# A three-stage Trainium2 kernel: eleven weight-half subtractions of the second group moved from GpSimd to VectorE, and to a later place

## The chip, the cores and the metric

The kernel runs on one core of a Trainium2 chip. The metric is the device time of one execution in microseconds (us). The engines are named as the profile names them: PE is TensorE (matmuls), PEld its weight load, DVE is VectorE, ACT is ScalarE, POOL is GpSimd, SP is the engine whose queue issues most DMAs. A "q" behind a name (SPq) is that engine's queue.

## What is computed

Three layers follow each other. The first is a linear attention with a decaying state over 2 batch rows, 8 heads, 768 steps and head size 48; the second and third are feed-forward layers of width 384 and 1024. In the excerpt the first two functions matter, since the change lies where they overlap.

```python
def _attn_ref(r, k, v, w, u):
    state = np.zeros((B, H, D, D))
    for t in range(S):
        cur = np.einsum('bhd,bhe->bhde', u[None] * kt, vt)
        y[:, :, t] = np.einsum('bhd,bhde->bhe', rt, state + cur)
        state = wt[:, :, :, None] * state + np.einsum('bhd,bhe->bhde', kt, vt)

def _moe_ref(x, mu_k, mu_r, w_k, w_v, w_r):
    xk = mu_k * x + (1.0 - mu_k) * x_prev
    xr = mu_r * x + (1.0 - mu_r) * x_prev
    k = np.maximum(xk @ w_k, 0.0)
    v = k * k @ w_v
    r = 1.0 / (1.0 + np.exp(-(xr @ w_r)))
    return r * v

def _moe2_ref(x, w_in, g_ln, w_sg, b_sg, w_out):
    h = gelu(x @ w_in); u, v = halves(h)
    v_s = w_sg @ normalised(v) + b_sg
    return x + (u * v_s) @ w_out
```

## The kernel before

The 1536 tokens are cut into four groups of 384 (half a batch row each). The attention of a group is done in four units, each a pair of heads over three chunks of 128 steps: units 0 to 3 are group 0, units 4 to 7 group 1, units 8 to 11 group 2. This text calls the ninth unit unit 8, as the code counts.

A unit has four stages on TensorE. S (`attn_sc`) transposes the scaled keys into `kt_ps`, from unit 8 on also sums the u-weighted products over a head into `ab`, and makes the scores `sc`. K (`attn_kv`) multiplies values with the keys' copy `kt` into `kv`. Y (`attn_y`) applies the masked scores `am`, and Z (`attn_z`) adds the carried state. Between them VectorE multiplies the masks in (`am<-sc`, two instructions, one for each head), forms `ru<-ab,uvt`, and steps the state (`zt`, `zcar`); ScalarE copies the keys out of PSUM (`kt<-kt_ps`, called the key eviction here) and scales the state into `sblk` and `scar`. `ab` and `kv` use the same PSUM buffer, so a unit's `kv` matmuls start only when `ru<-ab` has read it.

The second layer's products of a group stand between the stages of the next group's units: eight products k (`moe1_k`, here k0 to k7), three r, then three v in four parts each. In group 0 the weights are used whole. From group 1 on each weight and each input is a high half and a low half, and a product is three passes (high·high, low·high and high·low). For that the weights are split once, in `split1` and `split_to`: ScalarE copies the high half (`wh`, line 314) and another engine subtracts it from the full weight (`wkl`, `wrl`, `wvl`, line 315). The eight k weights are split on VectorE, the three r and eight v weights on GpSimd, all called from `moe1_v` when the last product of group 0 is written down. The k halves are needed by k0 of group 1, the r halves at its first r, the v halves at its first v.

Each k product is evicted by ScalarE with three instructions, `kr<-mm` (line 673), `kh<-kr` (686) and the square `kr<-kr` (687), and VectorE subtracts `kl<-kr,kh` (688). The inputs of the products are made in `moe1_prep` by `dx` on ScalarE (640) and VectorE (642), high halves `xkh` and `xrh` on ScalarE (645) and low halves `xkl` and `xrl` on VectorE (646).

The order on TensorE is written out by hand: a `plan` lists every stage and product, and `TS` gives the time that the plan expects for each. VectorE, ScalarE and the DMA queues are ordered by a scheduler from the priorities that `with at(time)` sets and from what is ready; `tc.issue_after(ins)` puts what a block issues on the engine of `ins` behind it in that engine's order, without a wait. Each engine runs its instructions in order. The low halves share a ring of buffers (tag `wl`) with the full weights, so a low half reuses the buffer of a weight split two places before it, and the third layer's weights (`stg<-w_in` loaded by SP, `top` on ScalarE, `wf` on VectorE) follow in the same ring. Three staging buffers hold these loads.

Of the kernel before, what the change touches and what calls it, by code (L numbers as in the profile page):

```python
# [13 lines left out]
AF = mybir.ActivationFunctionType  # L14
# [10 lines left out]
NP = H // 2  # L25
PW = 2 * D
HP = 64
PR = HP + D
WL = CG * (CH + 1) + 1
KM = DM // 128  # L30
# [30 lines left out]
NVN = 8  # L61
# [9 lines left out]
def emit(tc, tin, nin, vt, consts, ucp, pars, b_sg, w_k, w_v, w_r, w_in, w_sgT, w_out, outT):  # L71
    nc = tc.nc
    V, A, PL, PE, SP = nc.vector, nc.scalar, nc.gpsimd, nc.tensor, nc.sync
# [94 lines left out]
    TS, TE = {}, {}  # L168
# [53 lines left out]
    def wide(i):  # L222
        return i >= NP * N_DIAG
# [4 lines left out]
    def load_uvt(i):  # L228
        src = tin[subs[i // NP][0] * NP + i % NP]
        for q in rows(i == NP * N_DIAG):  # L230
            with at(TS["Y", i] - 9):
                SP.dma_start(uvts[q], src[q, WL + 2 * G:WL + 3 * G])
# [44 lines left out]
    def pair():  # L277
        return pl["w"].tile([128, 2 * WT + 2], U32 if early["n"] < N_EARLY else F32R, name="wh", tag="wh", bufs=NW1 // 2 + 1)
# [33 lines left out]
    def split_to(hi, lo, full, dl, e):  # L312
        with at(dl):
            i = A.activation(hi, full, AF.Copy).ins  # L314
            e.tensor_tensor(lo, full, hi.bitcast(F32), ALU.subtract)  # L315
        return i

    def full1(nm, i, shape):
        wt[nm, i] = (pl["w"].tile(shape, F32, name="w" + nm, tag="wl", bufs=NW1 + SPARE),)

    def split1(nm, i, dl, e=PL):
        if not split_ops[0]:
            return
        full = wt[nm, i][0]
        shape = list(full.shape)
        lo = pl["w"].tile(shape, F32R, name="w" + nm + "l", tag="wl", bufs=NW1 + SPARE)
        if early["hi"] % 2 == 0:
            early["t"] = pair()
        o = early["hi"] % 2 * WT
        early["hi"] += 1  # L330
        hi = early["t"][:, o:o + WT].rearrange("p (c f) -> p c f", c=shape[1])
        ins = split_to(hi, lo, full, dl, e)
        wt[nm, i] = (hi, lo)
        return ins
# [62 lines left out]
    st = {}  # L397
# [36 lines left out]
    def attn_sc(i):  # L434
        tS, tK, tY = TS["S", i], TS["K", i], TS["Y", i]
        s = st[i]
        nc_ = subs[i // NP][2]
        kt_ps = pq.tile([128, 512], F32, name="kt_ps", tag="kt", bufs=1)
        for c in range(nc_):
            PE.transpose(kt_ps[:, c * PR:(c + 1) * PR], s["kp"][:, c], ident[0:PR, 0:PR])  # L440

        def sums(bs):
            s["bs"] = bs
            for c in range(nc_):
                PE.matmul(bs[:, 2 * c:2 * c + 2], s["ruk"][:, c * CH:(c + 1) * CH], hm, start=True, stop=True)  # L445

        if i >= NP and not wide(i):
            sums(kt_ps[:, nc_ * PR:nc_ * PR + 2 * nc_])
        kt = pa.tile([128, nc_, PR], F32, name="kt", tag="ktsb")
        with at(tS + 0.5):  # L450
            A.activation(kt, kt_ps[:, 0:nc_ * PR].rearrange("p (c d) -> p c d", d=PR), AF.Copy)
        s["kt"] = kt
        am = pa.tile([128, 2, nc_, CH], F32, name="am", tag="am", bufs=B_AM)
        sc = [pq.tile([128, 512], F32, name="sc", tag="sc", bufs=2)[:, 0:nc_ * CH].rearrange("p (c t) -> p c t", t=CH)
              for _ in range(2)]
        if wide(i):
            ab = pq.tile([128, 512], F32, name="ab", tag="kv", bufs=1)[0:PR, 0:nc_ * CH]
            PE.matmul(ab, hblk, s["ruk"], start=True, stop=True)  # L458
        for c in range(nc_):
            for h in range(2):  # L460
                hs = slice(h * HP, h * HP + D)
                PE.matmul(sc[h][:, c], s["kp"][hs, c], s["rp"][hs, c], start=True, stop=True)  # L462
        if wide(i):
            with at(tK - 1.6):
                V.tensor_tensor(s["ruk"], ab, uvts, ALU.mult)
            if i + 1 < NU:
                load_uvt(i + 1)
            self_am(i, am, sc, tY)
            return
        if i < NP:  # L470
            sums(head["bs"][0][:, 0:2 * nc_])
        self_am(i, am, sc, tY)
        vb = pa.tile([128, nc_, 2, D], F32, name="vb", tag="vb", bufs=2)
        with at(tK - 1.6 if i >= NP else tY - 1.4):
            bh = s["bs"].rearrange("p (c h) -> p c h", h=2)[:, :, :, None].to_broadcast([128, nc_, 2, D])
            V.tensor_tensor(vb, uv[i].rearrange("p c (h d) -> p c h d", h=2), bh, ALU.mult)
        s["vb"] = vb

    def self_am(i, am, sc, tY):
        s = st[i]  # L480
        nc_ = subs[i // NP][2]
        for h in range(2):
            with at((TS["K", i] - 1.4 if i >= NP else tY - 1.2) + 0.4 * h):
                mask = cmask[:, None, :].to_broadcast([128, nc_, CH])
                s["am"] = V.tensor_tensor(am[:, h], sc[h], mask, ALU.mult).ins  # L485
        s["at"] = am
# [173 lines left out]
    def mm_tile():  # L660
        mmp["n"] += 1
        if mmp["q"] is not None and mmp["n"] % 8 >= 3:
            return mmp["q"].tile([128, 512], F32, name="mn", tag="mn", bufs=5)
        return pm.tile([128, 512], F32, name="mm", tag="mm", bufs=3)
# [35 lines left out]
    def moe1_v(s, j, q):  # L700
        g, c0, n = subs[s]
        js = slice(j * 128, (j + 1) * 128)
        if q == 0:
            m1[s, "ps"] = mm_tile()[:, 0:n * CH]
        ps = m1[s, "ps"]
        fs = range(q * KF // VQ, (q + 1) * KF // VQ)
        mm(ps, [(part(wt["v", f], slice(None), 0, js), m1[s, "k", f]) for f in fs], q == 0, q == VQ - 1)
        if q < VQ - 1:
            return
        with at(TE["v", s, j] - 0.5):  # L710
            V.tensor_tensor(x2[g][:, j, c0 * CH:(c0 + n) * CH], ps, m1[s, "r", j], ALU.mult)
        if s == NAT["r"] - 1 and j == KM - 1 and split_ops[0]:
            with tc.issue_after(st[2 * NP - 1]["ev"]):
                for f in range(KF):
                    hi = split1("k", f, TS["k", s + 1, f], V)
            with tc.issue_after(hi):
                for f in range(KM):
                    split1("r", f, TS["r", s + 1, f])
                for f in range(NVN):
                    split1("v", f, TS["v", s + 1, 0] + f * 0.49)  # L720

    m2 = {}

# [229 lines left out]
    def products(i):  # L953
        for _ in head["prep", i]:
            pass
# [14 lines left out]
    for n, key in enumerate(keys[:n_in]):  # L970
        kd, g = key[0], key[1]
# [40 lines left out]
        if kd == "S" and g >= UPIN - 1 and g + 1 < NU:  # L1012
            with tc.issue_after(st[g]["am"]):
                products(g + 1)
        if kd == "Z" and g >= NP and g + 2 < UPIN:
            prep(g + 2)
        elif kd == "Z" and g >= NP and g + 2 < NU:
            with tc.issue_after(st[g]["zt"]):
                scans(g + 2)
# [98 lines left out]
```

## Time and profile before

| what | us |
|---|---|
| median of 3 runs | 346.44 |
| lowest and highest of the 3 | 345.92, 348.27 |
| the profiled execution's own time | 346.58 |
| its span in the profile | 344.8 |

The span runs from the first to the last instruction that the profiler saw. The granted clock of TensorE was 0.998 of full speed over the span. A row of the timeline gives start, duration, engine, line, operation, output and inputs, count, and in brackets the engine's idle time before it with the work that the profile says ended it. That last name is an inference: where the named work had long been done, it was another.

### The profile page before, as it was taken

The page shows a single profiled execution, that of the slowest core. Times are in us where ns is not written, and L with a number is a line of the kernel's source. Part 1 is how long each engine was busy: PE and PEld are TensorE (multiplying, and loading weights), DVE is VectorE, ACT ScalarE, POOL GpSimd, SP SyncE. Part 2 cuts the span into 40 slices and gives each one's busy share as a digit, 9 for nine tenths or more (in the row PEclk, how much of TensorE's full clock was granted, in tenths as well). Part 3 has the DMA queues.
Part 4 walks back from the last instruction along what each step waited for, and adds up shares of the span by engine and source line. Part 5 has one row for each costly group of instructions (what it writes and reads, how often), then busy time and mean ns, then how long its engine had stood idle before and what let it go on. Part 6 is the DMA issues. An engine that isn't in the chain of part 4 may idle for free.

```text
span 344.8 us, 5996 instructions
## 1 busy us (share of the span) xinstructions
PE 332.2 (96%) x2179; PEld 289.9 (84%) x2179; DVE 243.7 (71%) x531; ACT 182.6 (53%) x430; POOL 32.9 (10%) x56
## 2 busy tenths in 40 slices
PE   7999999999978999999999999999999999999993
PEld 3776577676767889888899999989999999999992
DVE  5997899789968883699439652498989732645531
ACT  3474986537789751777438892868353206211100
POOL 3000000001750000000004053000000000000000
PEclk9999999999999999999999999999999999999999
DMA  8788963754224430011013423613330010100012
GB/s 223 191 286 252 310 181 110 202 134 129 96 61 135 117 108 19 18 27 44 19 63 94 136 86 107 216 25 80 78 82 20 1 70 0 46 25 0 2 73 75
DMA packets 23750, 33.97 MB, mean 99 GB/s; under 512 B 3504, under 2 KB 18032, under 8 KB 23712
## 3 DMA queue, kind: packets, MB, share of 16 engines
q1 hardware_dynamic: 21568, 31.09, 31.3%
q10 hardware_dynamic: 2144, 2.41, 2.4%
q8 instruction: 19, 0.31, 0.4%
q14 instruction: 19, 0.16, 0.2%
HBM read 28.77 MB, written 2.36 MB: 90 GB/s over the span
## 4 chain that ended last, share of the span: by engine, by line
PE 85%; DVE 5%; ACT 4%; DMA 3%; issue 1%; POOL 0%; SPq 0%; DVEq 0%; ACTq 0%; POOLq 0%
PE mm L606 41%; PE mn L606 27%; PE sc L462 4%; PE y L545 3%; PE y L559 3%; ACT wh L314 2%; DMA wh<-w_r 2%; PE kv L501 2%; PE y L548 1%; PE kt_ps L440 1%; PE ab L458 1%; DMA uw<-tin 1%; PE mm L937 1%; PE kt_ps L445 1%; DVE dx L642 1%
## 5 line engine op out<-in xcount | busy, mean ns | idle before, releaser
L594 ACT ACTIVATE gah<-gt 128x384 fp32r<-128x384 f32 x16 | 8.4, 526 | 44.4 <-DVE gt L787 44.4
L640 ACT ACTIVATE dx<-xx,par 128x384 f32<-128x384 f32 x22 | 13.3, 611 | 22.0 <-DMA xx<-yo 19.9
L527 ACT ACTIVATE sblk<-zt,pf 48x48 f32<-48x48 f32 x60 | 19.8, 331 | 9.4 <-DVE zt L511 6.6
L606 PE MATMUL mm<-kh,wh 128*128 128x384 f32 x64 | 22.1, 346 | 0.0
L606 PE MATMUL mm<-kh,wvl 128*128 128x384 f32 x64 | 21.6, 337 | 0.0
L606 PE MATMUL mm<-kl,wh 128*128 128x384 f32 x64 | 21.5, 336 | 0.0
L606 PE MATMUL mm<-xkh,wh 128*128 128x384 f32 x57 | 20.3, 357 | 0.0
L606 PE MATMUL mn<-wsh,vl 128*128 128x384 f32 x60 | 20.0, 334 | 0.0
L606 PE MATMUL mn<-wsh,vh 128*128 128x384 f32 x60 | 20.0, 334 | 0.0
L606 PE MATMUL mn<-wsl,vh 128*128 128x384 f32 x60 | 20.0, 334 | 0.0
L688 DVE TENSOR_TENSOR kl<-kr,kh 128x384 fp32r<-128x384 f32 x24 | 15.3, 636 | 6.1 <-ACT kr L687 6.1
L606 PE MATMUL mm<-xkl,wh 128*128 128x384 f32 x57 | 19.3, 338 | 0.2 <-DVE xkl L646 0.2
L606 PE MATMUL mm<-xkh,wkl 128*128 128x384 f32 x57 | 19.2, 337 | 0.0
L315 POOL TENSOR_TENSOR w2l<-wf,w2h 128x384 fp32r<-128x384 f32 x12 | 12.9, 1088 | 63.9 <-ACT w2h L314 63.9
L417 DVE TENSOR_TENSOR_SCAN pf<-uw,d1f 112x387 f32<-112x387 f32 x16 | 15.3, 957 | 3.3 <-DMA uw<-tin 2.5
L673 ACT ACTIVATE kr<-mm 128x384 f32<-128x384 f32 x27 | 12.9, 478 | 8.5 <-PE mm L606 8.3
L485 DVE TENSOR_TENSOR am<-sc,cst 128x384 f32<-128x384 f32 x32 | 16.3, 547 | 1.4 <-PE sc L462 1.4
L545 PE MATMUL y<-am,uv 128*48 128x128 f32 (+1 forms) x192 | 15.6, 277 | 1.7 <-DVE am L485 1.6
L606 PE MATMUL mm<-xkh,wk 128*128 128x384 f32 x48 | 17.0, 497 | 0.0
L606 PE MATMUL mm<-kh,wv 128*128 128x384 f32 x48 | 16.3, 490 | 0.0
L462 PEld LDWEIGHTS sc<-rp,kp 48*128 48x128 f32 x192 | 12.0, 187 | 5.1 <-issue 4.5
L642 DVE SCALAR_TENSOR_TENSOR dx<-xx,par,dx 128x384 f32<-128x384 f32 x18 | 13.8, 776 | 3.0 <-ACT dx L640 3.0
(215 smaller groups left out, 980.3 us busy)
## 6 DMA issues: line engine op xcount, KB each, us to landing
urk<-tin SPq DMA_DIRECT2D x26, 144.0 KB, 3.6
wh<-w_k SPq DMA_DIRECT2D x8, 384.0 KB, 3.8
stg<-w_in SPq DMA_DIRECT2D x8, 384.0 KB, 3.5
wq<-tin SPq DMA_DIRECT2D x16, 168.0 KB, 2.4
wsf<-w_sgT SPq DMA_DIRECT2D x12, 192.0 KB, 3.4
outT<-ot SPq DMA_DIRECT2D x12, 192.0 KB, 1.9
uv<-nin ACTq DMA_DIRECT2D x14, 144.0 KB, 3.3
uw<-tin SPq DMA_DIRECT2D x26, 72.8 KB, 3.5
```

The lines of the kernel that those rows point to most:

```text
L315: e.tensor_tensor(lo, full, hi.bitcast(F32), ALU.subtract)
L417: V.tensor_tensor_scan(pf[:, 0:n1], w[:, 0:n1], d1f[:, 0:n1], 1.0, ALU.mult, ALU.max)
L462: PE.matmul(sc[h][:, c], s["kp"][hs, c], s["rp"][hs, c], start=True, stop=True)
L485: s["am"] = V.tensor_tensor(am[:, h], sc[h], mask, ALU.mult).ins
L527: A.activation(sb[hs, hs], o[hs], AF.Copy, scale=s["pe"][c][hs])
L545: PE.matmul(y3[hs, c], uv[i][:, c, h * D:PW if h else HP], s["at"][:, h, c], start=(c == 0), stop=False, skip_group_check=True)
L559: PE.matmul(y3[0:PR, c], s["us"][c], s["rp"][:, c], start=False, stop=(c == cs[-1]), skip_group_check=True)
L606: PE.matmul(ps, l, r, start=(first and k == 0), stop=(last and k == len(prods) - 1))
L640: A.activation(d, xj[:, 1 + t0:1 + t1], AF.Copy, scale=mu[:, j:j + 1])
L642: V.scalar_tensor_tensor(ops[0][:, j] if nat else d, xj[:, t0:t1], nu[:, j:j + 1], d, ALU.mult, ALU.add)
L673: m1[s, "ev", f] = A.activation(kr, ps, AF.Relu).ins
L688: V.tensor_tensor(kl, kr, kh.bitcast(F32), ALU.subtract)
```

## The change

The r and v weights of group 1 on are no longer split in `moe1_v` but in a new function, `split_rv`, called once after stage K of unit 8. The subtractions run on VectorE. Two `issue_after` blocks put what it issues behind the second mask multiplication of unit 8 on VectorE and behind unit 8's key eviction on ScalarE; the latter's instruction is kept in `s["ka"]` for that. The split of the k weights stays where it was.

```diff
+    def split_rv(s):
+        with tc.issue_after(st[s * NP]["am"]), tc.issue_after(st[s * NP]["ka"]):
+            for f in range(KM):
+                split1("r", f, TS["r", s, f], V)
+            for f in range(NVN):
+                split1("v", f, TS["v", s, 0] + f * 0.49, V)
+
...
         with at(tS + 0.5):
-            A.activation(kt, kt_ps[:, 0:nc_ * PR].rearrange("p (c d) -> p c d", d=PR), AF.Copy)
+            s["ka"] = A.activation(kt, kt_ps[:, 0:nc_ * PR].rearrange("p (c d) -> p c d", d=PR), AF.Copy).ins
...
             with tc.issue_after(st[2 * NP - 1]["ev"]):
                 for f in range(KF):
-                    hi = split1("k", f, TS["k", s + 1, f], V)
-            with tc.issue_after(hi):
-                for f in range(KM):
-                    split1("r", f, TS["r", s + 1, f])
-                for f in range(NVN):
-                    split1("v", f, TS["v", s + 1, 0] + f * 0.49)
+                    split1("k", f, TS["k", s + 1, f], V)
...
+        if kd == "K" and g == 2 * NP:
+            split_rv(g // NP)
```

TensorE's order is the same in both kernels. On GpSimd the eleven subtractions are gone and nothing else moves. The rows below are pieces of an engine's instruction order, before and after; line numbers shift by 7 in the changed kernel.

VectorE around unit 8's masks. `kl` belongs to k0, k1 and later k products, `am` are the masks, `zt` and `zcar` the state steps, `wf` the first third-layer weight. Before:

```order
L688 TENSOR_TENSOR kl<-kr,kh 128x384
L465 TENSOR_TENSOR ru<-ab,uvt 112x384
L485 TENSOR_TENSOR am<-sc,cst 128x384
L688 TENSOR_TENSOR kl<-kr,kh 128x384
L485 TENSOR_TENSOR am<-sc,cst 128x384
L511 COPY zt<-kv 112x48
L310 SCALAR_TENSOR_TENSOR wf<-stg,top_128 128x384
L513 SCALAR_TENSOR_TENSOR zt<-zt,pf,kv 112x48
```

After:

```order
L695 TENSOR_TENSOR kl<-kr,kh 128x384
L472 TENSOR_TENSOR ru<-ab,uvt 112x384
L695 TENSOR_TENSOR kl<-kr,kh 128x384
L492 TENSOR_TENSOR am<-sc,cst 128x384 x2
L315 TENSOR_TENSOR wrl<-wr,wh 128x384 x2
L518 COPY zt<-kv 112x48
L315 TENSOR_TENSOR wrl<-wr,wh 128x384
L520 SCALAR_TENSOR_TENSOR zt<-zt,pf,kv 112x48
L315 TENSOR_TENSOR wvl<-wv,wh 128x384
L520 SCALAR_TENSOR_TENSOR zcar<-zt,pf,kv 112x48
L315 TENSOR_TENSOR wvl<-wv,wh 128x384 x2
```

Both masks now stand behind the second `kl`, the subtractions follow the masks with the state steps between them, and `wf` has left this place.

VectorE around unit 9's masks (`yo` is unit 8's output, `ru<-ab` unit 9's). Before:

```order
L688 TENSOR_TENSOR kl<-kr,kh 128x384
L569 TENSOR_TENSOR yo<-y,ru 112x384
L465 TENSOR_TENSOR ru<-ab,uvt 112x384
L431 SCALAR_TENSOR_TENSOR ru<-urk_109,cst 112x384
L688 TENSOR_TENSOR kl<-kr,kh 128x384
L485 TENSOR_TENSOR am<-sc,cst 128x384 x2
```

After:

```order
L576 TENSOR_TENSOR yo<-y,ru 112x384
L695 TENSOR_TENSOR kl<-kr,kh 128x384
L472 TENSOR_TENSOR ru<-ab,uvt 112x384
L438 SCALAR_TENSOR_TENSOR ru<-urk_109,cst 112x384
L315 TENSOR_TENSOR wvl<-wv,wh 128x384
L695 TENSOR_TENSOR kl<-kr,kh 128x384
L492 TENSOR_TENSOR am<-sc,cst 128x384 x2
L315 TENSOR_TENSOR wvl<-wv,wh 128x384
```

One v subtraction, the eighth of the eleven, stands ahead of unit 9's masks; three follow them.

ScalarE from the last input copies to unit 8's key eviction (`kt`) and behind it. Before:

```order
L645 ACTIVATE xrh<-dx 128x384
L314 ACTIVATE wh<-wv 128x384
L673 ACTIVATE kr<-mm 128x384
L645 ACTIVATE xrh<-dx 128x384
L686 ACTIVATE kh<-kr 128x384
L314 ACTIVATE wh<-wv 128x384
L687 ACTIVATE kr<-kr 128x384
L673 ACTIVATE kr<-mm 128x384
L451 ACTIVATE kt<-kt_ps 128x336
L686 ACTIVATE kh<-kr 128x384
L314 ACTIVATE wh<-wv 128x384
L687 ACTIVATE kr<-kr 128x384
```

After:

```order
L308 ACTIVATE top_128<-stg 128x384
L652 ACTIVATE xrh<-dx 128x384
L308 ACTIVATE top_127<-stg 128x384
L652 ACTIVATE xrh<-dx 128x384
L680 ACTIVATE kr<-mm 128x384
L693 ACTIVATE kh<-kr 128x384
L694 ACTIVATE kr<-kr 128x384
L680 ACTIVATE kr<-mm 128x384
L458 ACTIVATE kt<-kt_ps 128x336
L693 ACTIVATE kh<-kr 128x384
L314 ACTIVATE wh<-wr 128x384
L694 ACTIVATE kr<-kr 128x384
```

The r and v high halves have left the evictions of k0 and k1, two `top` copies of the third layer have come forward to there, and the first r high half stands ahead of k1's square.

## Rows read from the trace of the kernel before

**Rows 1.** Page, part 1: busy us, share of the span, instructions.
```profile
PE 332.2 (96%) x2179; PEld 289.9 (84%) x2179; DVE 243.7 (71%) x531; ACT 182.6 (53%) x430; POOL 32.9 (10%) x56
```
**Rows 2.** Windows: length, busy (instructions) of PE, PEld, DVE, ACT, POOL; clock, DMA, GB/s.
```profile
99.00:104.60 5.60, 5.60 (x41) 4.89 (x39) 2.36 (x4) 4.12 (x11) 1.54 (x2) 1.00 0.35 99
115.00:338.90 223.90, 223.90 (x1374) 212.91 (x1372) 145.46 (x335) 106.37 (x243) 15.99 (x25) 1.00 0.21 60
```
**Rows 3.** Timeline of PE, units 8, 9 and 10: start us, us, then the instruction.
```profile
89.50 0.45 PE L606 MATMUL mm<-xkl,wh 128*128 128x384 f32 x1 [0.21 <-DVE xkl L646]
...
91.81 0.81 PE L458 MATMUL ab<-ru,hblk 112*112 112x384 f32 x2
...
94.92 0.34 PE L606 MATMUL mm<-xkh,wkl 128*128 128x384 f32 x1
96.68 0.52 PE L501 MATMUL kv<-uv,kt 128*64 128x48 f32 x12 [1.43 <-ACT kr L687]
...
98.26 0.86 PE L545 MATMUL y<-am,uv 128*48 128x128 f32 x10 [0.73 <-DVE am L485]
99.05 0.44 PE L606 MATMUL mm<-xkh,wh 128*128 128x384 f32 x1
...
106.11 0.34 PE L606 MATMUL mm<-xkh,wkl 128*128 128x384 f32 x1
106.71 0.52 PE L501 MATMUL kv<-uv,kt 128*64 128x48 f32 x12 [0.25 <-ACT top L308]
108.12 1.32 PE L545 MATMUL y<-am,uv 128*64 128x128 f32 x12 [0.90 <-DVE am L485]
109.37 0.44 PE L606 MATMUL mm<-xkh,wh 128*128 128x384 f32 x1
...
116.47 0.33 PE L606 MATMUL mm<-xrh,wrl 128*128 128x384 f32 x1
116.73 0.49 PE L501 MATMUL kv<-uv,kt 128*64 128x48 f32 x11
...
117.88 0.44 PE L606 MATMUL mm<-xrh,wh 128*128 128x384 f32 x1
```
**Rows 4.** Timeline of DVE, 83 to 98 us.
```profile
83.65 1.96 DVE L315 TENSOR_TENSOR wkl<-wk,wh 128x384 fp32r<-128x384 f32 x4
85.52 2.62 DVE L642 SCALAR_TENSOR_TENSOR dx<-xx,par,dx 128x384 f32<-128x384 f32 x2
88.07 1.38 DVE L646 TENSOR_TENSOR xkl<-dx,xkh 128x384 fp32r<-128x384 f32 x1
89.37 1.36 DVE L646 TENSOR_TENSOR xrl<-dx,xrh 128x384 fp32r<-128x384 f32 x1
90.66 0.60 DVE L642 SCALAR_TENSOR_TENSOR dx<-xx,par,dx 128x384 f32<-128x384 f32 x1
...
92.25 2.59 DVE L646 TENSOR_TENSOR xrl<-dx,xrh 128x384 fp32r<-128x384 f32 x2
94.76 1.35 DVE L688 TENSOR_TENSOR kl<-kr,kh 128x384 fp32r<-128x384 f32 x1
96.04 0.55 DVE L465 TENSOR_TENSOR ru<-ab,uvt 112x384 f32<-112x384 f32 x1
...
96.97 0.77 DVE L688 TENSOR_TENSOR kl<-kr,kh 128x384 fp32r<-128x384 f32 x1
```
**Rows 5.** Timeline of POOL: six of the first seven of the eleven subtractions.
```profile
85.31 3.72 POOL L315 TENSOR_TENSOR wrl<-wr,wh 128x384 fp32r<-128x384 f32 x3 [47.69 <-DVE wkl L315]
...
91.93 3.77 POOL L315 TENSOR_TENSOR wvl<-wv,wh 128x384 fp32r<-128x384 f32 x3 [1.61 <-ACT wh L314]
```
**Rows 6.** Timeline of ACT: the high halves of the k weights.
```profile
80.75 3.40 ACT L314 ACTIVATE wh<-wk 128x384 fp32r<-128x384 f32 x8
```
**Rows 7.** Timeline of SP: the first three loads of third-layer weights.
```profile
83.66 1.38 SPq L297 DMA_DIRECT2D stg<-w_in  x3
```
**Rows 8.** Page, part 6: KB of one load, median us from issue to landing.
```profile
stg<-w_in SPq DMA_DIRECT2D x8, 384.0 KB, 3.5
```

## The prediction

> **What bounds the kernel now.** I read the page's busy shares first: TensorE is busy for 332.2 us of the span, and no other engine comes near [rows 1]. The windows say more: from 115.0 to 338.9 TensorE is busy for all of 223.9 us at a granted clock of 1.00 [rows 2]. So nothing that the change touches later than 115 can give time, and any time that TensorE gains before 115 reaches the end whole, since its order stays the same. The question is what it loses between 87 and 115, and for that I read its timeline around the K and Y stages of units 8 and 9, with unit 10 as the undisturbed pattern [rows 3].
>
> In unit 10 the first `kv` starts 0.26 behind the last product's last matmul (116.47 to 116.73), and the next product starts 1.15 behind that (117.88). Against this pattern:
>
> - k0 waits 0.21 for `xkl` (the row at 89.50).
> - Unit 8: 94.92 to 96.68 is 1.76, so 1.50 lost ahead of `kv`; 96.68 to 99.05 is 2.37, so 1.22 lost in Y.
> - Unit 9: 106.11 to 106.71 is 0.60, so 0.34 lost; 106.71 to 109.37 is 2.66, so 1.51 lost in Y.
>
> The sum is 4.78 us, and no edit here can give back more than that. The row at 96.68 names ScalarE's square, but `kv` shares its buffer with `ab`, and the instruction that reads `ab`, `ru`, ran from 96.04 to 96.59 on VectorE [rows 4]: `kv` started 0.09 later. So unit 8 waits for VectorE twice, first for `ru`, then for the masks.
>
> **Why VectorE is late there.** VectorE's timeline shows the same instructions at two durations. The k subtractions take 1.96 for four, 0.47 from one start to the next and 0.55 for one alone; a `dx` at 90.66 takes 0.60. But two `dx` at 85.52 take 2.62, `xkl` 1.38, `xrl` 1.36, two more `xrl` 2.59, `kl` 1.35 and 0.77 [rows 4]. The long ones lie in GpSimd's busy stretches, 85.31 to 89.03 and 91.93 to 95.70, the short `dx` starts in the gap between them [rows 5]. The excess is 1.42 + 0.83 + 0.81 + 1.49 + 0.80 + 0.22 = 5.57 us on an engine that had no pause there.
>
> The Trainium skill ("SBUF — State Buffer", section "Who interferes with whom") says that a VectorE instruction with two SBUF inputs contends with a GpSimd instruction that reads SBUF, and that the one that issues second is blocked until the first is done. The trace agrees on which instructions suffer; on the size it gives less than a whole GpSimd subtraction (3.72 / 3 = 1.24), some 0.8 for one. It makes the last rival below less likely.
>
> **The change part by part.**
>
> *GpSimd's eleven subtractions go.* VectorE's 5.57 excess goes with them. `xkl`: the last four k subtractions start at 83.65 and take four steps of 0.47, two `dx` 1.20, `xkl` 0.55, so it is ready at about 87.3, two us before TensorE asks (89.29). The 0.21 goes. What is late next for unit 8 is no longer VectorE's backlog but TensorE's own `ab` (91.81 + 0.81 - 0.21 = 92.4 [rows 3]); `ru` follows at 92.5 and is done at 93.0. `kv` could start at 94.92 - 0.21 + 0.26 = 94.97. The 1.50 goes, with two us to spare.
>
> *Both masks of unit 8 now stand behind k1's `kl`,* and this waits for ScalarE. ScalarE's step between 128x384 instructions is 3.40 / 8, so 0.41 with the last one 0.51 [rows 6]. VectorE's exchange with ScalarE over the inputs (`dx`, `xrh`, `xrl`) ends near 91 without the excess, so ScalarE reaches k0's eviction at about 90.4: three steps to 91.6, then k1's `kr`, the key eviction, `kh`, one r half, and the square ends near 93.75. A hand-over costs 0.05 (`xkl` ends at 89.45, TensorE goes on at 89.50 [rows 3, 4]). So `kl` at 93.8, masks at 94.27 and 94.74, done at 95.3. TensorE wants them 0.4 to 0.5 after 94.97. I take 0.1 of the 1.22 as staying; at the bounds 0 and 1.0, the latter if ScalarE comes a microsecond late.
>
> *The two `top` copies* ahead of k0's eviction need two loads. The three were issued between 83.66 and 85.04 [rows 7], landing takes 3.5 [rows 8], so all are there by 88.5, when ScalarE gets to the first. Its pauses for VectorE's `dx` hide them: nothing. With later landings k0's eviction pays up to 1.0, which is the bound just given.
>
> *Eleven subtractions on VectorE* are 11 x 0.47 = 5.2 us. Seven fall behind unit 8's masks, where VectorE was busy only 2.36 of 5.60 us [rows 2], one stands ahead of unit 9's masks, three behind. Here the path is again ScalarE's. The product after unit 8, k3, starts at 94.97 + 1.15 = 96.1. Unit 9's `kv` is free 106.11 + 0.26 - 99.05 = 7.32 later, at 103.4, and the masks are wanted from 103.85. From the square's start at 93.25 ScalarE runs it and five weight halves to 95.7, then seven more full steps and six short state copies; the latter at a little less than 0.41 (an estimate), k4's `kr` starts near 100.6, and with key eviction, `kh`, one v half and the square, VectorE gets k4's square at 102.75. Then `kl`, two masks, done at 104.3. TensorE waits 0.4 of the 1.51 + 0.34 that it lost before; with the short copies at the full 0.41 it would be 0.8. The v subtraction there waits for its own high half (ready at 102.3), so it ends before the square comes.
>
> *`wf` and the third-layer loads behind it* go later, past subtractions and a scan. On SP the fourth load now waits for the first `wf` with one state load and unit 9's output transfer behind it, but VectorE's order has `wf` ahead of unit 9's output, so that transfer is not held. ScalarE's fourth `top` may stand until that load lands, while TensorE has over 4 us of work ahead of its next need (r products, stage Z). Nothing, and the cover is this.
>
> *Unit 10:* the same count puts its masks 0.1 to 0.2 ahead of TensorE. Nothing.
>
> Sum: 4.78 - 0.1 - 0.4 = 4.3 us less. The profiled execution took 346.58, 0.14 above the median, so 342.3 from it and 342.1 from the median; I forecast 342.2.
>
> **The rivals.**
>
> *Half the gain.* Unit 8 recovers, but unit 9's masks stay as late against TensorE as they were, because VectorE and ScalarE, in order and with more between them, hand the lateness on. For it: seven VectorE subtractions each wait for a ScalarE half, and the chain of unit 9 has no slack. Against it: the count above. Price: 4.78 - 0.1 - 1.85 = 2.8, so 343.7.
>
> *Nothing:* a wait of the same size takes their place, with `top` standing for its load ahead of k0's eviction and unit 10's masks late by an r product as well. It needs several late things at once; under 1 us is left, about 346.
>
> *Slower.* VectorE's long durations are not GpSimd's doing but something of the place (ScalarE's or DMA's traffic). Then unit 8's loss stays, and eight more subtractions at up to 1.30 stand ahead of unit 9's masks: 10.4 against 5.60 - 2.36 = 3.24 of pause there, 7.2 us, up to 353.6; at 0.47 each it is 0.5. It decides from 0.41 for each subtraction on. Against it stand the short `dx` in GpSimd's gap and the GpSimd stretches that fit the long ones. The Trainium skill ("Perfetto Trace Analysis", section "Optimizing Scalar/DVE Operations") says that with VectorE saturated, offloading work even to GpSimd may make sense, and adds that between those two it might not help; by its first half the change goes the wrong way, and this rival is what it would do. The trace bears out the second half. I take 348.5 for it.
>
> **How the numbers follow.** The forecast has 0.64, half the gain 0.23, nothing 0.07, slower 0.06. About 1% (3.5 us) is what a measurement of this kernel can tell from no change: below 343.0 is faster. A little of the half-gain case falls there, a little of the forecast's falls out: faster 0.65, same 0.29, slower 0.06. The lower end, 341.4, is the whole 4.78 and 0.3 for the spread between executions; the upper end, 344.6, takes in most of the half-gain case.
>
> **What would show it.** In the changed kernel's profile GpSimd runs no r or v subtraction, all VectorE instructions of 128x384 between 85 and 100 take 0.55 to 0.61, k0 has no wait, unit 8's `kv` follows k2 within 0.3, k3 starts near 96.1 and k6 near 105. The forecast is wrong if long VectorE instructions remain (slower), if TensorE waits over 1 us in Y of unit 9 (half), or if a gap opens at k3 to k5 that was not there, for a PSUM buffer whose eviction stands behind the `top` copies.

## The result and the profile after

The changed kernel takes 342.16 us (median of four runs, 342.03 to 342.25) against 347.14 for the kernel before (four runs, 345.92 to 348.27): a ratio of 0.9861, 95% interval 0.9829 to 0.9893. It is faster by 1.4%; the forecast was 342.2. Between the two profiled executions (346.58 and 342.25) the gain is 4.3; the medians give 5.0, since the kernel before scatters more. Two of the profiles below are of executions that took longer than most of their kernel (343.90 and 344.66 us): in both, TensorE's granted clock was lower between 30 and 50 us (0.92 and 0.91, 0.97 and 0.86 in its two halves), ahead of the stretch that is compared, so only distances within that stretch are read from them.

Page, part 1, of the changed kernel (busy us, share of the span, instructions):

```profile
PE 332.3 (98%) x2179; PEld 290.3 (85%) x2179; DVE 242.3 (71%) x542; ACT 182.1 (53%) x430; POOL 19.6 (6%) x45
```

Against [rows 1] TensorE's busy time is the same to 0.1 us. GpSimd lost eleven instructions and 13.3 us. VectorE got these eleven, and yet is busy for 1.4 us less: the instructions that it already had became shorter by more than the new ones cost.

Timeline of TensorE, units 8, 9 and 10 (start us, us, then the instruction; line numbers are 7 higher than before):

```profile
87.41 0.63 PE L613 MATMUL mm<-xkh,wh 128*128 128x384 f32 x1
...
90.83 0.45 PE L447 MATMUL kt_ps<-cst,kp 112*128 112x112 f32 x3
...
94.22 0.34 PE L613 MATMUL mm<-xkh,wkl 128*128 128x384 f32 x1
94.49 0.55 PE L508 MATMUL kv<-uv,kt 128*64 128x48 f32 x12
...
95.88 0.44 PE L613 MATMUL mm<-xkh,wh 128*128 128x384 f32 x1
...
102.94 0.34 PE L613 MATMUL mm<-xkh,wkl 128*128 128x384 f32 x1
103.21 0.55 PE L508 MATMUL kv<-uv,kt 128*64 128x48 f32 x12
...
105.03 0.44 PE L613 MATMUL mm<-xkh,wh 128*128 128x384 f32 x1
...
112.16 0.33 PE L613 MATMUL mm<-xrh,wrl 128*128 128x384 f32 x1
112.42 0.55 PE L508 MATMUL kv<-uv,kt 128*64 128x48 f32 x12
...
113.71 0.44 PE L613 MATMUL mm<-xrh,wh 128*128 128x384 f32 x1
```

These are the places of [rows 3], and the same pattern serves as the ruler: last product to `kv` 0.26, `kv` to the next product 1.15. `kv` now follows at 0.27, 0.27 and 0.26, so nothing is lost in any K stage. In Y, unit 8 takes 95.88 - 94.49 = 1.39 (0.24 lost), unit 9 takes 1.82 (0.67 lost), unit 10 takes 1.29 (0.14 lost). For the whole stretch two more rows of TensorE's timeline of before are needed, k0's start and the start of unit 8's S stage:

```profile
87.61 0.63 PE L606 MATMUL mm<-xkh,wh 128*128 128x384 f32 x1
...
91.52 0.45 PE L440 MATMUL kt_ps<-cst,kp 112*128 112x112 f32 x3
```

From k0's start to the first product behind unit 10's Y stage it was 117.88 - 87.61 = 30.27, and it is 113.71 - 87.41 = 26.30: 3.97 us gained in the stretch that the prediction spoke of. k0 itself starts 0.20 earlier, and the rest of the span's 344.8 - 340.4 = 4.4, some 0.2, comes behind the stretch; where these two come from no run shows.

Timeline of VectorE in the same stretch:

```profile
86.38 0.56 DVE L653 TENSOR_TENSOR xkl<-dx,xkh 128x384 fp32r<-128x384 f32 x1
...
91.58 0.56 DVE L695 TENSOR_TENSOR kl<-kr,kh 128x384 fp32r<-128x384 f32 x1 [0.93 <-ACT kr L694]
92.06 0.55 DVE L472 TENSOR_TENSOR ru<-ab,uvt 112x384 f32<-112x384 f32 x1
93.54 0.56 DVE L695 TENSOR_TENSOR kl<-kr,kh 128x384 fp32r<-128x384 f32 x1 [0.93 <-ACT kr L694]
94.02 1.02 DVE L492 TENSOR_TENSOR am<-sc,cst 128x384 f32<-128x384 f32 x2
...
100.69 0.56 DVE L695 TENSOR_TENSOR kl<-kr,kh 128x384 fp32r<-128x384 f32 x1 [0.38 <-ACT kr L694]
101.17 0.55 DVE L472 TENSOR_TENSOR ru<-ab,uvt 112x384 f32<-112x384 f32 x1
101.63 0.61 DVE L438 SCALAR_TENSOR_TENSOR ru<-urk,cst 112x384 f32<-112x384 f32 x1
102.23 0.56 DVE L315 TENSOR_TENSOR wvl<-wv,wh 128x384 fp32r<-128x384 f32 x1
102.71 0.55 DVE L695 TENSOR_TENSOR kl<-kr,kh 128x384 fp32r<-128x384 f32 x1
103.18 1.02 DVE L492 TENSOR_TENSOR am<-sc,cst 128x384 f32<-128x384 f32 x2
...
111.38 0.56 DVE L695 TENSOR_TENSOR kl<-kr,kh 128x384 fp32r<-128x384 f32 x1 [0.46 <-ACT kr L694]
111.85 1.02 DVE L492 TENSOR_TENSOR am<-sc,cst 128x384 f32<-128x384 f32 x2
```

Where [rows 4] has `xkl` at 1.38 and `kl` at 1.35, both now take 0.56, and VectorE pauses ahead of `kl` (0.93, for ScalarE's square): before, ScalarE was waiting for it. Ahead of unit 9's masks it has no pause: from 100.69 to 103.18 five instructions stand back to back, among them a v subtraction and k4's `kl`, which TensorE does not need then. In all three units the next product starts 0.83 or 0.84 behind the end of the second mask: 95.04 to 95.88, 104.20 to 105.03, 112.87 to 113.71. With the ruler's 1.15 that sets when TensorE wants the second mask: 0.31 behind `kv`'s start. Windows of the two stretches that [rows 2] shows of before (PE, PEld, DVE, ACT, POOL busy, granted clock, DMA):

```profile
95.88:101.45 5.57, 5.57 (x41) 4.89 (x40) 4.78 (x13) 5.42 (x16) 0.00 (x0) 1.00 0.11 29
110.75:334.40 223.65, 223.65 (x1371) 212.96 (x1372) 145.56 (x336) 107.16 (x246) 16.01 (x25) 1.00 0.21 62
```

Behind 110.75 TensorE is as full as before. Between unit 8's Y stage and unit 9's first product behind its scores VectorE went from 2.36 busy us to 4.78, and this costs TensorE nothing: it takes 5.57 us for this stretch in both kernels (95.88 to 101.45, and 99.05 to 104.62 before).

### The profile page after: what moved, and what is told of

Read it like the earlier page. It is cut to its first block, busy times and chain, and to the rows that moved or that the text cites. A ratio compares the mean times of both kernels' runs of the same rounds, so it can differ in the third digit from the quotient of the medians.

```text
span 340.4 us, 5990 instructions
## 1 busy us (share of the span) xinstructions
PE 332.3 (98%) x2179; PEld 290.3 (85%) x2179; DVE 242.3 (71%) x542; ACT 182.1 (53%) x430; POOL 19.6 (6%) x45
## 3 DMA queue, kind: packets, MB, share of 16 engines
HBM read 28.77 MB, written 2.36 MB: 91 GB/s over the span
## 4 chain that ended last, share of the span: by engine, by line
PE 92%; DVE 3%; DMA 1%; ACT 1%; issue 1%; SPq 0%; DVEq 0%
PE mm L613 45%; PE mn L613 28%; PE sc L469 4%; PE y L552 3%; PE mm L939 3%; PE y L566 3%; PE kv L508 2%; PE ab L465 2%; DMA xx<-yo 1%; PE kt_ps L447 1%; PE y L555 1%; PE mm L452 1%; PE kt_ps L452 1%; DVE am L492 0%; DVE wk L310 0%
## 5 line engine op out<-in xcount | busy, mean ns | idle before, releaser
L695 DVE TENSOR_TENSOR kl<-kr,kh 128x384 fp32r<-128x384 f32 x24 | 14.3, 598 | 8.1 <-ACT kr L694 8.1
L429 DVE TENSOR_TENSOR_SCAN pr<-uw,d1r 112x387 f32<-112x387 f32 x16 | 15.4, 963 | 0.4
```

The source lines that it names most:

```text
L429: V.tensor_tensor_scan(pr[:, 1:wl][:, ::-1], w[:, 1:wl][:, ::-1], dr[:, 1:wl][:, ::-1], 0.0, ALU.mult, ALU.add)
L695: V.tensor_tensor(kl, kr, kh.bitcast(F32), ALU.subtract)
```

## Experiments

The change does two things at once: it takes the subtractions from GpSimd to VectorE, and it takes them to a later place. Theory A says that the first is the cause: GpSimd's reads make VectorE's instructions long. Theory B says the second is: the subtractions and their halves on ScalarE stood in the way where they were. The first four runs, on one chip beside 19 runs of the kernel before (median 346.78), tell these apart.

**VectorE at the old place.** The diff is against the kernel before. Nothing else that runs is changed in the code; the scheduler shifts some of VectorE's and ScalarE's other instructions with it.

```diff
                 for f in range(KM):
-                    split1("r", f, TS["r", s + 1, f])
+                    split1("r", f, TS["r", s + 1, f], V)
                 for f in range(NVN):
-                    split1("v", f, TS["v", s + 1, 0] + f * 0.49)
+                    split1("v", f, TS["v", s + 1, 0] + f * 0.49, V)
```

> The engine alone is changed: the eleven subtractions run on VectorE, but are issued from the old place (behind the k split), so six of them and ScalarE's r and v high halves stand ahead of unit 8's masks. Theory A (contention): what cost time was VectorE's instructions with two SBUF inputs running at 1.3 us beside GpSimd's subtractions; without GpSimd they take 0.55 to 0.62, the 5.6 us of excess go, 6 x 0.47 = 2.8 us come back ahead of the masks: 342.8 to 344.5 us, most of the gain stays. Theory B (place): what counts is that the subtractions and high halves leave the stretch ahead of unit 8's masks, whatever the engine: 345.5 to 347 us, nearly nothing stays.

Measured: 341.66 (341.40 to 341.73, four runs), ratio 0.9844 [0.9804, 0.9883]. The whole gain is there without the new place, and half a microsecond more than that. The expectation by theory A, 342.8 to 344.5, was too high: it priced the six subtractions ahead of unit 8's masks at 2.8 us, and unit 8 loses no more than in the changed kernel. Its timelines, VectorE and TensorE at unit 9:

```profile
102.00 0.55 DVE L492 TENSOR_TENSOR am<-sc,cst 128x384 f32<-128x384 f32 x1
102.56 0.56 DVE L695 TENSOR_TENSOR kl<-kr,kh 128x384 fp32r<-128x384 f32 x1
103.04 0.55 DVE L492 TENSOR_TENSOR am<-sc,cst 128x384 f32<-128x384 f32 x1
```
```profile
103.02 0.55 PE L508 MATMUL kv<-uv,kt 128*64 128x48 f32 x12
...
104.43 0.44 PE L613 MATMUL mm<-xkh,wh 128*128 128x384 f32 x1
```

Here no v subtraction is left to stand ahead of unit 9's masks, and `kl` stands between the two, not ahead of both. `kv` to the next product is 1.41 in unit 9 (0.26 lost, against 0.67), 1.36 in unit 8 and 1.15 in unit 10: 0.47 lost in all, against 1.05 in the changed kernel. So theory B falls; the later place costs some 0.6.

**GpSimd at the new place.** The diff is against the changed kernel.

```diff
             for f in range(KM):
-                split1("r", f, TS["r", s, f], V)
+                split1("r", f, TS["r", s, f])
             for f in range(NVN):
-                split1("v", f, TS["v", s, 0] + f * 0.49, V)
+                split1("v", f, TS["v", s, 0] + f * 0.49)
```

> The place alone is changed: the subtractions stay on GpSimd, but are issued behind unit 8's masks and key eviction. Theory A (contention): unit 8 is as in the changed kernel (k3 starts near 96), but VectorE's instructions with two SBUF inputs between 93 and 107 (kl of k2 to k5, ru from urk) take 1.2 to 1.4 us, unit 9's masks are later by one or two such excesses of 0.8: 342.8 to 344.2 us. Theory B (place): the same as the changed kernel, 341.8 to 342.6 us.

Measured: 344.24 (344.00 to 348.67, ten runs), ratio 0.9935 [0.9896, 0.9974]: 2.1 us over the changed kernel. Its timelines, GpSimd, then VectorE, then ScalarE and TensorE:

```profile
92.91 3.26 POOL L315 TENSOR_TENSOR wrl<-wr,wh 128x384 fp32r<-128x384 f32 x3 [56.12 <-ACT wh L314]
96.13 4.24 POOL L315 TENSOR_TENSOR wvl<-wv,wh 128x384 fp32r<-128x384 f32 x4
102.06 4.24 POOL L315 TENSOR_TENSOR wvl<-wv,wh 128x384 fp32r<-128x384 f32 x4 [1.70 <-ACT wh L314]
```
```profile
93.28 1.07 DVE L695 TENSOR_TENSOR kl<-kr,kh 128x384 fp32r<-128x384 f32 x1 [0.93 <-ACT kr L694]
...
105.36 1.83 DVE L310 SCALAR_TENSOR_TENSOR wf<-stg,top 128x384 uint32<-128x384 uint32 x2 [1.39 <-POOL wvl L315]
```
```profile
106.75 0.65 ACT L308 ACTIVATE top<-stg 128x384 f16<-128x384 bf16 x1 [2.70 <-DVE wf L310]
```
```profile
114.77 0.85 PE L552 MATMUL y<-am,uv 128*48 128x128 f32 x10 [0.94 <-DVE am L492]
```

A's size was about right, its place was not. `kl` is long beside GpSimd (1.07) and costs unit 8's Y stage 1.90 - 1.39 = 0.51 more; unit 9 is better by 0.46 (103.45 to 104.81, 1.36), as no v subtraction stands on VectorE ahead of its masks and `kl` stands between them. Most of the price comes later and by another way: `wf` reuses a buffer of the ring and waits for GpSimd's last `wvl` but one, then takes 1.36 beside the last, ScalarE's next `top` waits 2.70 for `wf`, and the state copies and evictions queue behind that `top`. The scheduler has a part in this: it put `wf` ahead of unit 9's state steps and `top` ahead of k5's `kh`, where in the changed kernel both stand later. So this run is not the change of one engine alone. From unit 9's next product to r0 TensorE takes 6.48 against 5.62, and unit 10's Y stage 2.51 against 1.29. The sum is 0.51 - 0.46 + 0.86 + 1.22 = 2.13. `kv` of unit 8 starts 0.27 earlier (94.22), which leaves 1.86; the spans differ by 342.2 - 340.4 = 1.8, the medians by 2.1.

**GpSimd reads that nobody waits for.** The changed kernel with eleven GpSimd subtractions added at the old place, of a k weight half from itself, into a tile that is overwritten later. The orders of the other engines are those of the changed kernel, so only GpSimd's work differs.

```diff
+            k7 = wt["k", KF - 1][0].bitcast(F32).rearrange("p c f -> p (c f)")
+            for _ in range(KM + NVN):
+                PL.tensor_tensor(xx[NG - 1][:, 0, 1:1 + G], k7, k7, ALU.subtract)
```

> The changed kernel, with eleven more subtractions on GpSimd that read an already split k half twice and write a place in the last group's input that is overwritten later; nobody waits for them, and the order of every other engine is that of the changed kernel. They run from about 84 to 97 us. Theory A (contention): VectorE's instructions with two SBUF inputs take about 1.3 us again between 84 and 97, the queue ahead of unit 8's masks grows by 5 us or more, of which its pauses for ScalarE (1 to 2 us) hide a part: 344.5 to 347 us. Theory B (place): nothing waits for GpSimd, so 341.8 to 342.6 us.

Measured: 346.77 (345.75 to 349.48, ten runs), ratio 0.9997 [0.9969, 1.0026]. The whole gain is gone. Timelines of GpSimd, VectorE and TensorE, and windows of the stretch behind unit 8's last product:

```profile
84.11 12.11 POOL L725 TENSOR_TENSOR xx<-wh 128x384 f32<-128x384 f32 x11 [46.62 <-ACT wh L314]
```
```profile
88.86 1.18 DVE L653 TENSOR_TENSOR xkl<-dx,xkh 128x384 fp32r<-128x384 f32 x1
...
92.16 0.55 DVE L718 TENSOR_TENSOR xx<-mm,rs 128x384 f32<-128x384 f32 x1
```
```profile
90.09 0.45 PE L613 MATMUL mm<-xkl,wh 128*128 128x384 f32 x1 [0.93 <-DVE xkl L653]
...
97.21 0.52 PE L508 MATMUL kv<-uv,kt 128*64 128x48 f32 x12 [1.36 <-ACT wh L314]
...
99.95 0.69 PE L613 MATMUL mm<-xkh,wh 128*128 128x384 f32 x1
100.43 0.52 PE L613 MATMUL mm<-xkl,wh 128*128 128x384 f32 x1
```
```profile
95.30:99.90 4.60, 2.48 (x28) 1.51 (x26) 4.33 (x10) 4.60 (x13) 0.93 (x1) 0.95 0.12 32
99.90:103.00 3.10, 3.10 (x11) 3.06 (x11) 2.79 (x9) 2.67 (x8) 0.00 (x0) 0.53 0.00 0
```

VectorE's instructions with both inputs in SBUF take 1.18 with 1.10 from start to start, and GpSimd's eleven take 12.11, which is the same step of 1.10: VectorE gets one such instruction done for each of GpSimd's. `xx<-mm` at 92.16 has one input in PSUM and stays at 0.55. Against the changed kernel TensorE loses 1.21 at `xkl` (two steps, 88.82 to 90.37, take 1.55, where 0.34 would do), 1.43 ahead of unit 8's `kv` (95.51 to 97.21 is 1.70, against 0.27) and 1.35 in unit 8's Y stage (2.74 against 1.39). Then it goes on at a granted clock of 0.53, the 1.2 GHz level, after a stretch in which it was busy for 2.48 of 4.60 us: matmuls of 0.52 instead of 0.34, 6.86 to unit 9's next product against 5.57, 1.29 lost. Unit 9's masks are ready in the meantime and give 0.55 back (1.27 against 1.82). The sum is 4.73, the spans differ by 345.2 - 340.4 = 4.8.

**GpSimd writes in the same place.** As the last one, but a memset of the same tile in place of each subtraction, and one small subtraction ahead to place them in time.

```diff
+            PL.tensor_tensor(xx[NG - 1][:, 0, 1:17], k7[:, 0:16], k7[:, 0:16], ALU.subtract)
+            for _ in range(KM + NVN):
+                PL.memset(xx[NG - 1][:, :, 1:1 + G], 0.0)
```

> As the run with extra subtractions, but the eleven GpSimd instructions are memsets of 128 x 1152 values, which read nothing. Theory A in the form of the Trainium skill (SBUF - State Buffer, Who interferes with whom: contention only with a GpSimd instruction that reads SBUF): 341.8 to 342.6 us, VectorE's instructions stay at 0.55 to 0.62. A wider theory C (any GpSimd instruction on SBUF slows VectorE): long VectorE instructions as in the run with subtractions, 344 to 347 us.

Measured: 342.25 (341.96 to 342.36, four runs), ratio 0.9859 [0.9819, 0.9899]: the changed kernel's time. GpSimd and VectorE:

```profile
84.58 12.24 POOL L726 MEMSET xx<- 128x1152 f32 x11
```
```profile
86.38 0.55 DVE L653 TENSOR_TENSOR xkl<-dx,xkh 128x384 fp32r<-128x384 f32 x1
```

GpSimd is busy as long and over the same stretch, and VectorE runs at 0.55. So it is GpSimd's reads that matter, not that it works. The Trainium skill ("SBUF — State Buffer", section "Who interferes with whom") says just this: a VectorE instruction with two SBUF inputs contends with a GpSimd instruction that reads SBUF and not with one that only writes it. These two runs agree on both halves, 346.77 and 342.25.

**What is left in unit 9: ScalarE's halves?** The next runs, on another chip (kernel before 346.33, eleven runs), ask where the 0.67 of unit 9 come from. Theory D puts it on the ScalarE halves that now stand between the key products' evictions, theory E on VectorE, which has eight subtractions between unit 8's masks and unit 9's. The edit makes the eleven halves at the old place and leaves the subtractions at the new one:

```diff
-                    split1("k", f, TS["k", s + 1, f], V)
+                    hi = split1("k", f, TS["k", s + 1, f], V)
+            with tc.issue_after(hi):
+                halves_rv(s + 1)
...
-        with tc.issue_after(st[s * NP]["am"]), tc.issue_after(st[s * NP]["ka"]):
-            for f in range(KM):
-                split1("r", f, TS["r", s, f], V)
-            for f in range(NVN):
-                split1("v", f, TS["v", s, 0] + f * 0.49, V)
+        with tc.issue_after(st[s * NP]["am"]):
+            for nm, i, dl in rv(s):
...
+                with at(dl):
+                    V.tensor_tensor(lo, full, hi.bitcast(F32), ALU.subtract)
```

> The changed kernel, but ScalarE makes the r and v high halves at the old place (behind the k halves); VectorE's subtractions stay behind unit 8's masks. Theory D (ScalarE): what the changed kernel still loses in Y of unit 9 (0.67 us) is that a v half and its subtraction stand ahead of k4's square and kl in the two queues; with the halves gone from there TensorE does not wait for unit 9's masks, and the time is that of the run with the old place, 341.3 to 341.9 us. Theory E (VectorE): it is the eight subtractions between unit 8's and unit 9's masks, which stay: 342.0 to 342.4 us.

Measured: 342.03 (341.56 to 343.90, six runs), ratio 0.986 [0.9825, 0.9896]. Unit 9's `kv` to the next product is 106.77 - 105.07 = 1.70, so 0.55 is still lost there with no half in ScalarE's way: for unit 9 D falls. VectorE runs without a pause from 100.64, three v subtractions ahead of unit 8's output, then another `kl`, `ru`, k4's `kl` at 104.45 and both masks behind it at 104.92. But units 8 and 10 lose nothing in this run (1.15 from `kv` to the next product in each, with one of the two masks now ahead of a `kl`), so 0.55 is lost in all, against 1.05. Three of the six runs (341.56 to 341.64) lie below every run of the changed kernel on this chip (342.13 and more). So the halves' late place, with the orders that came with it, costs some 0.5, only not where D looked for it.

**The v part later still.** r behind unit 8's masks as in the changed kernel, v behind unit 9's.

```diff
-        if kd == "K" and g == 2 * NP:
-            split_rv(g // NP)
+        if kd == "K" and g in (2 * NP, 2 * NP + 1):
+            split_rv(g // NP, "rv"[g - 2 * NP], g)
```

> The changed kernel, but only the r split stands behind unit 8's masks, and the v split behind unit 9's masks and key eviction. Both theories D and E expect that unit 9's masks are no longer waited for (0.67 us back), but six v halves then stand ahead of k5's eviction and the v subtractions between unit 9's and unit 10's masks, so unit 10 pays: by theory D 0.7 to 1.5 us there, 342.0 to 343.2 us; by theory E about what unit 9 paid before, 342.0 to 342.3 us; if neither queue matters there, 341.4 to 341.8 us.

Measured: 342.99 (342.47 to 344.79, six runs), ratio 0.9894 [0.9858, 0.9929]. Unit 9 is well (1.34, 0.19 lost, no v subtraction ahead of its masks), and unit 10 pays:

```profile
112.97 1.32 PE L552 MATMUL y<-am,uv 128*64 128x128 f32 x12 [0.32 <-DVE am L492]
```

`kv` started at 112.10 and the next product at 114.22, 2.12, so 0.97 is lost in unit 10. Its masks went from 111.85 to 112.37, and both engines have a part in that. ScalarE runs six v halves from 102.06 ahead of a key product's eviction (104.55 against 103.75), and another at 110.75 ahead of the square that unit 10's `kl` waits for; that square ends at 111.68, against 111.34 in the changed kernel. On VectorE four v subtractions stand between 107 and 112, the last of them directly ahead of that `kl`, which starts at 111.91. So some 0.3 of the 0.5 is ScalarE's, as D had it: its range for this run, 342.0 to 343.2, holds, and E's, 342.0 to 342.3, does not. The lateness moves one unit further and grows.

**Old place against new, again.** The first experiment's kernel and the changed kernel, six runs each on the same chip as the last two.

> The same kernel as the run with VectorE at the old place, next to the changed kernel on one chip: 341.4 to 341.8 us, 0.4 to 0.6 us less than the changed kernel, if the late place costs time in unit 9 as both theories D and E say; the same as the changed kernel if the earlier difference was one of chips.

> The changed kernel as it is, on the same chip as the three runs beside it: 342.0 to 342.3 us; it is the mark for differences of half a microsecond.

Measured: 341.57 (341.36 to 342.54), ratio 0.9848 [0.9816, 0.9879], and 342.36 (342.13 to 342.69), ratio 0.9866 [0.9835, 0.9897]. Five of the six runs at the old place lie below every run of the changed kernel; at the medians the difference is 0.8 on this chip, where 0.4 to 0.6 was expected. The profile loses what the first one lost, 0.21 in unit 8 and 0.26 in unit 9. The plain move to VectorE beats both kernels.

**Masks ahead of `kl`.** Theory F: what is left in unit 9 is the order on VectorE, where the masks stand behind k4's `kl`. The edit raises the masks' priority in the changed kernel, and the one thing that it changes in any engine's order is that unit 9's masks come ahead of that `kl`.

```diff
-            with at((TS["K", i] - 1.4 if i >= NP else tY - 1.2) + 0.4 * h):
+            with at((TS["K", i] - (4.4 if i in (8, 9, 10) else 1.4) if i >= NP else tY - 1.2) + 0.4 * h):
```

> The changed kernel with one difference in any engine's order: on VectorE both masks of unit 9 stand ahead of k4's kl, not behind it (the masks' scheduling time is set 3 us earlier for units 8 to 10; nothing else moves). Theory F: what the changed kernel still loses in Y of unit 9 (0.67 us) is that the masks stand behind a kl that waits for ScalarE's square. The masks then start behind the v subtraction, near 102.7 and 103.2 instead of 103.18 and 103.65, TensorE's wait falls from 0.67 to 0.1 to 0.3, and the time to 341.6 to 341.9 us. Theory E (VectorE is full there): 342.1 to 342.4 us, as the changed kernel.

> The changed kernel once more, as the mark on this chip for the run beside it: 342.0 to 342.4 us.

Measured on a third chip: 341.82 (341.69 to 344.66, seven runs), ratio 0.9857 [0.9826, 0.9888], beside the changed kernel at 342.38 (341.92 to 344.78, six runs), ratio 0.9895 [0.9854, 0.9936]. VectorE at unit 9:

```profile
105.23 1.01 DVE L492 TENSOR_TENSOR am<-sc,cst 128x384 f32<-128x384 f32 x2
106.16 0.55 DVE L695 TENSOR_TENSOR kl<-kr,kh 128x384 fp32r<-128x384 f32 x1
```

`kv` to the next product is 107.08 - 105.73 = 1.35: 0.20 lost in place of 0.67, a difference of 0.47, and 0.47 is VectorE's step for one `kl`. F holds for unit 9, and E, which expected no gain, falls there. Unit 10 gives a part back: 115.93 - 114.45 = 1.48, so 0.33 is lost there, where it was 0.14. That leaves 0.29 in the three units. The medians differ by 0.56, less than their spread, so the size rests on the timeline.

**The kernel before, once more,** with a profile, to see whether its losses are the same from one execution to the next.

> The kernel before, for a second profile. Its runs spread from 345.9 to 350.6 us, those of the changed kernel by less than 1 us. If the spread comes from TensorE's granted clock falling behind the pauses that the change shortens, a profile of a longer execution shows a stretch of granted clock near 0.5 between 95 and 112; if not, it shows another place or none. At about 346 us it should look as the first profile does.

Measured: 346.22, against 346.58 in the first profile. Windows of this second profile:

```profile
95.00:99.00 4.00, 1.82 (x26) 1.36 (x25) 3.12 (x6) 3.99 (x11) 3.36 (x4) 0.97 0.16 37
99.00:103.00 4.00, 4.00 (x15) 4.00 (x16) 2.36 (x4) 2.54 (x8) 1.33 (x2) 0.60 0.28 84
```

Unit 8 loses what it lost in [rows 3]: `kv` 1.77 behind the last product, where it was 1.76, and the next product 2.40 behind, where it was 2.37. Then TensorE runs at a granted clock of 0.60, where the first profile has 1.00 [rows 2] (at this time the second was expected to look like the first), and unit 9 waits for hardly anything: 0.27 ahead of `kv` and 1.48 in Y, so 0.34 lost, against 1.85. The slower clock took up the time in which TensorE would have waited for unit 9's masks. No longer execution of this kernel was profiled, so why some take 348 to 350 us stays open.

The same window of the first profile, for the last section:

```profile
95.00:99.00 4.00, 1.84 (x26) 1.22 (x24) 3.32 (x6) 3.99 (x12) 3.37 (x4) 1.00 0.14 37
```

## Why the prediction was right

- *No other stretch matters.* Right: behind 110.75 TensorE has no pause in the changed kernel, and the time gained ahead of that reached the end whole. GpSimd still has twelve other subtractions (`w2l`, 176 to 207 us) that lengthen VectorE's instructions, a `dx` to 1.38, and TensorE does not wait there.
- *Why VectorE is late: GpSimd's reads.* Right, and shown from both sides: taken away at the old place they give the gain (341.66), added to the changed kernel they take it away (346.77), and writes do nothing (342.25). One reading was incomplete: `xrl` at 89.37 and `kl` at 96.97 don't lie in the two stretches of GpSimd that the prediction names, but in two that [rows 5] leaves out:

```profile
89.25 1.07 POOL L315 TENSOR_TENSOR wvl<-wv,wh 128x384 fp32r<-128x384 f32 x1 [0.22 <-ACT wh L314]
...
96.33 4.22 POOL L315 TENSOR_TENSOR wvl<-wv,wh 128x384 fp32r<-128x384 f32 x4 [0.63 <-ACT wh L314]
```

  The gap with the short `dx` is the one from 90.32 to 91.93, so the argument stands. The blocking that the prediction takes from the Trainium skill ("SBUF — State Buffer") stands there in another section than the one named, "Summary: rules for kernel authors": of a VectorE instruction with two SBUF inputs and a GpSimd one that reads SBUF, the second to issue is blocked until the first finishes. The trace agrees, and with this it gives the size too, where the prediction found less than a whole GpSimd subtraction: `xkl` ends at 89.45, `xrl` at 90.73 and `kl` at 96.11, and the GpSimd instructions beside them at 89.03, 90.32 and 95.70, 0.41 or 0.42 earlier each time. A VectorE instruction waits out what is left of GpSimd's when it starts, not a whole one. The `kl` at 96.97, with 0.36 left of GpSimd's (the first of the four ends at 97.33), took only 0.77.
- *k0.* The prediction took the 0.21 of the idle column; 0.49 came back. From k0's start to unit 8's first transpose it was 91.52 - 87.61 = 3.91 and is 90.83 - 87.41 = 3.42. The waiting matmul started 0.38 behind its place in the row of products, and took 0.28 to the next one instead of 0.17. A pause costs more than its bracket says: the bracket counts from the end of the matmul before, and in a row of products a matmul of 0.34 is followed by the next after 0.17. So the 4.78 that the prediction called the most an edit could give back was 0.28 too low.
- *Unit 8, K.* Right: 1.50 forecast, 1.49 come back, `ru` at 92.06 against the forecast 92.5 and `kv` 0.27 behind the last product.
- *Unit 8, Y.* 0.1 forecast to stay, 0.24 stayed. `kl` of k1 started at 93.54 (forecast 93.8) and the masks at 94.02 (94.27), done at 95.04 (95.3); the forecast's order of waits was right. The masks were 0.26 ahead of the forecast, but `kv` was 0.48 ahead of it, at 94.49 in place of 94.97.
- *The two `top` copies* did not hold k0's eviction: ScalarE ran it at 89.97, ahead of the forecast 90.4. Whether they have a part in unit 8's 0.24 no run shows.
- *`wf` and the loads behind it* cost nothing, as forecast: ScalarE's fourth `top` ran at 111.25 with no pause ahead of it.
- *Unit 9.* Its K stage gave back the whole 0.34. Of Y 0.67 stayed where 0.4 was forecast. The term had the chain right: it followed ScalarE to k4's square (forecast 102.75, the square ended at 102.61) and put `kl` and the masks behind it, done at 104.20 (forecast 104.3). The v subtraction, which the prediction took as done before that, held `kl` by little: it started at 102.71, 0.10 behind the square's end, and 0.05 of that is the hand-over. What was mis-sized is TensorE's side. It wants the second mask 0.31 behind `kv`, where the prediction took 0.45 (103.4 to 103.85): 0.14. `kv` came at 103.21, 0.19 ahead of the forecast, and the masks only 0.10: 0.09. The rest of the 0.27 is that 0.45 was rounded to 0.4. Of what stayed, 0.47 is `kl` itself, which TensorE did not need there.
- *Unit 10.* 0 forecast, 0.14 lost: its masks too stood behind a `kl`, at 111.38, ahead of which VectorE waited 0.46 for ScalarE.
- *The sum.* 4.3 forecast, 3.97 in the stretch: 0.28 more at k0, 0.14, 0.27 and 0.14 less in the three Y stages, with rounding in the rest. 0.4 came from outside the stretch, and the span shrank by 4.4. So the total, 342.16 against 342.2, was closer than its parts, and that is luck: the terms were off by 0.1 to 0.3 each, both ways.
- *The rivals.* Half the gain would have needed unit 9 as late as before (1.85 lost there, 0.67 came). Nothing would have needed k0's eviction held by `top`, and it came early. Slower would have needed VectorE's long durations to stay; none did in this stretch. The edit's second half, the later place, was no part of the gain: the prediction priced its cost at 0.5 us in unit 8 and 9 and did not ask what the kernel would do without it. It does 0.5 to 0.8 us better.

## What to carry to other kernels

When an engine that TensorE waits for shows the same instruction at two durations, lay its timeline beside the others' and look which one is busy in the long ones; here eleven GpSimd subtractions that nobody waited for cost 4.5 us (346.77 against 342.25 with memsets in their place). Work taken from GpSimd to an engine that is already the late one can pay if what it removes from each of that engine's own instructions is more than what it adds. Try such a move first without a new place: each later place put something ahead of some unit's masks, and who shares a ring of buffers with the moved work waits for it as well.

## What the hardware showed beyond that

- A VectorE instruction of 128x384 with two SBUF inputs that starts while GpSimd runs a subtraction ends 0.41 or 0.42 us behind the end of that one. This holds for all 24 of them between 84 and 107 us in three profiles: nine in the kernel before, four with GpSimd at the new place, eleven with the extra reads. So its length goes by what is left of GpSimd's instruction: 1.36 with 0.95 left, 1.18 with 0.76 left, 0.71 with 0.30 left, and 0.55 to 0.62 with no GpSimd subtraction beside it. Instructions with one input in PSUM beside the same subtractions keep 0.54 to 0.56.
- TensorE's granted clock fell to 0.53 and 0.60 in the windows shown, towards the 1.2 GHz level, for some 3 us (matmuls of 0.52 to 0.69 from 99.95 to 102.67 and from 98.86 to 101.91) right behind a stretch in which it had been busy for 2.48 of 4.60 and 1.82 of 4.00 us. In the first profile of the kernel before TensorE had paused as much, 1.84 busy us of the same 4.00, and its clock stayed at 1.00 behind it [rows 2].
- Such a slow stretch isn't always added to the time. In the second profile of the kernel before it stood where TensorE would have waited, and 346.22 came out in place of 346.58. In the run with GpSimd reads it cost 1.29 and gave back 0.55 of it.
